# First expert's last low parts go from VectorE to GpSimd, and two table sums go behind the gathered rows

## The chip, the cores and the metric

The kernel runs on one core of one Trainium2 chip. The metric is the device time of one execution in microseconds (us), lower is better. Engines are named as the profile names them: PE (TensorE matmul), PEld (its weight loads), DVE (VectorE), ACT (ScalarE), POOL (GpSimd), SP (SyncE, which issues most DMAs).

## What is computed

Three layers in a row, all in float32, on 1536 tokens of width 512:

```python
x = attention(q, k, v)          # window of 16 keys on each side, and 24 block summaries
h = x @ w_in                    # 512 -> 2048
x2 = elu(h) @ w_out             # 2048 -> 512
logits = x2 @ w_gate            # 8 experts, each token goes to its best one
gate = softmax(logits)[best]
out[i] = gate[i] * (relu(x2[i] @ w1[e]) @ w2[e])     # e = best[i], at most 384 tokens per expert
```

Float32 products are made of "fp32r" matmuls: an operand is split into a high part (a cast, on ACT) and a low part (operand minus high part, one TENSOR_TENSOR subtraction on DVE or POOL), and three matmul passes add high x high, high x low and low x high.

## The kernel before

The tokens are taken in four tiles of 384. Attention and the two dense matmuls fill the first 350 us. Behind them come the experts, and the change lies in the stretch between, from 357 to 375 us of the profiled span. The program is written out by hand in one order for each engine: code that stands earlier is earlier in the engine's queue, and an instruction waits for the semaphores of what it reads.

Three strands run side by side there.

The first strand is the *first expert's first block*. The expert with the most tokens in the first three tiles is chosen early. Its 16 weight chunks E_0 to E_15 (128x512 each; E_0 to E_7 are of w1, E_8 to E_15 of w2) come by DMA into six `rawq` buffers, and `conv_expert` splits each: `conv_hi` is a cast on ACT (L668), `conv_lo` a subtraction (L678) on DVE, or on POOL for the chunks listed in `pool`. `Block.first` multiplies the block's rows by E_0 to E_7 (L736, tiles bh0f and bh1f), `Block.turn` transposes the result (L744) and casts its high part (L746), `turn_lo` makes its low part on DVE (L753, tile hTf), and `Block.second` multiplies by E_8 to E_15 (L760, tile yf).

The second strand is the *routing of the last tile* (`route`, a generator whose pieces are run by `next(last)`): logits (lgT, the copy ls at L523, lg), then a chain of small DVE steps on 128x24 elements that finds each token's expert (L531 to L574; `oh` at L568 marks it, `cum` at L574 counts), the matmuls pp (L581) that read `oh`, a second chain of DVE steps (L588 to L612), the matmul tp (L619), and `tab` (L626), the table of token numbers by expert and position.

The third strand is the *rest of the first expert*: from `tab` the DVE makes `gidxa`, the row numbers (L1307 to L649); POOL issues two indirect DMAs that gather those rows (L693, tile xgq); PE transposes them (L700, tile bt), ACT casts the high part (L703, tile xbq) and DVE makes the low part (L704). Then every engine loads two token counts from `regs` into registers (TENSOR_LOAD) and branches, and PE multiplies the gathered rows by E_0 and so on (L810, tile bh): first eight passes that read only the high part of xbq, then four that read its low part.

Between these, the DVE counts tokens (`count_key`, L633), sorts the other seven experts by size (L1338 to L1370, ending in `regs`), and POOL and DVE bring the table into sorted order: `by_rank(v)` is a multiplication on POOL (L1358, tile tmp), and a sum on DVE follows for each v (L1379, tile tabs). `regs` also lets SP load expert numbers and start the DMAs of the next expert's weights.

Of the kernel before, what the change touches and what calls it, by code (L numbers as in the profile page):

```python
# [49 lines left out]
def build(tc, cap, qT, kT, vT, vP, wi, wo, wg, wgT, wx, out):  # L50
# [6 lines left out]
    with ctx:  # L57
        pool = lambda **kw: ctx.enter_context(tc.tile_pool(**kw))
# [569 lines left out]
        def count_key(nm, n):  # L628

            ct = psm("ct" + nm, "T")  # L630
            nc.tensor.matmul(ct[:, 0:NE], lhsT=ones, rhs=cums[n], start=True, stop=True)
            cnt = const.tile([P, NE], F32, name="cnt" + nm)
            nc.vector.tensor_copy(cnt, ct[:, 0:NE])  # L633
            key = const.tile([P, NE], F32, name="key" + nm)
            nc.vector.tensor_scalar(out=key, in0=cnt, scalar1=float(NE), scalar2=None, op0=ALU.mult)
            nc.vector.tensor_tensor(key, key, iota_e, op=ALU.subtract)
            return cnt, key

        def slots(src, n, nm):

            gidx = const.tile([P, n], U32, name="gidx" + nm)
            nc.vector.tensor_scalar(out=gidx, in0=src[:, :, 0], scalar1=1.0, scalar2=-1.0, op0=ALU.max, op1=ALU.add)
            gate = const.tile([P, n], F32, name="gate" + nm)
            nc.vector.tensor_tensor(gate, src[:, :, 1], src[:, :, 2], op=ALU.add)
            pad = const.tile([P, n], F32, name="pad" + nm)
            nc.vector.tensor_scalar(out=pad, in0=src[:, :, 0], scalar1=0.0, scalar2=padid, op0=ALU.is_equal, op1=ALU.mult)
            nc.vector.tensor_tensor(pad, pad, src[:, :, 0], op=ALU.add)
            sidx = const.tile([P, n], U32, name="sidx" + nm)
            nc.vector.tensor_scalar(out=sidx, in0=pad, scalar1=-1.0, scalar2=None, op0=ALU.add)  # L649
            return gate, gidx, sidx  # L650
# [4 lines left out]
        NCHUNK = 16  # L655
# [3 lines left out]
        def raw_of(k, m):  # L659
            return RAW[m % NRAW] if k == 0 else RAW[((k - 1) * NCHUNK + m) % len(RAW)]  # L660

        def raw_load(k, ms):
            for m in ms:
                nc.sync.dma_start(raw_of(k, m), wx[ds(ereg[k], 1), :, m, :].rearrange("o p f -> p (o f)"))

        def conv_hi(k, ms, vec=()):
            for m in ms:
                (nc.vector.tensor_copy if m in vec else nc.scalar.copy)(EW[k][m][:, 0], raw_of(k, m))  # L668

        def conv_expert(k, ms, pool=(), vec=()):  # L670
            for m in ms:
                conv_hi(k, [m], vec)
                conv_lo(k, [m], pool)

        def conv_lo(k, ms, pool=()):
            for m in ms:
                w, raw = EW[k][m], raw_of(k, m)
                (nc.gpsimd if m in pool else nc.vector).tensor_tensor(w[:, 1], raw, w[:, 0].bitcast(F32), op=ALU.subtract)  # L678
                nxt = m + len(RAW)
                if nxt < NCHUNK:  # L680
                    raw_load(k, [nxt])
                elif 0 < k < NE - 1:
                    raw_load(k + 1, [nxt - NCHUNK])

        def alloc_expert(k):

            pl, tg = (wpool, "W") if k % 2 == 0 else (w2pool, "W2")
            EW[k] = [pl.tile([P, 2, 512], F32R, tag=tg, name=f"E{k}_{m}") for m in range(NCHUNK)]
            for i in range(k + 2, NE, 2):
                EW[i] = EW[k]  # L690
# [6 lines left out]
        def load_xT(xb, col, xg, nm):  # L697
            pt = psm("bt" + nm, "TSO"[col // P])
            for c in range(NCC):
                nc.tensor.transpose(pt[:, c * P : (c + 1) * P], xg[:, c * P : (c + 1) * P], ident)  # L700
            ptv = pt.rearrange("p (c q) -> p c q", q=P)
            q = slice(col, col + P)
            nc.scalar.copy(xb[:, 0, :, q], ptv)  # L703
            nc.vector.tensor_tensor(xb[:, 1, :, q], ptv, xb[:, 0, :, q].bitcast(F32), op=ALU.subtract)  # L704
# [169 lines left out]
        def busy(n):  # L874

            warm = pacc("warm")
            for _ in range(n):
                nc.tensor.transpose(warm[:, 0:P], ident, ident)
# [395 lines left out]
        next(last)  # L1274
        blk.first(0, 2)
        blk.first(0, 3)
        conv_expert(0, range(11, 12))
        next(last)
        blk.turn(0, lo=False)
        blk.first(1, 0)  # L1280
        conv_hi(0, range(12, NCHUNK))
        next(last)
        blk.turn_lo(0)
        blk.first(1, 1)
# [3 lines left out]
        blk.second(0)  # L1288
        blk.second(1)
        blk.turn(1, lo=False)  # L1290
        conv_lo(0, range(12, 13))
        next(last, None)
        blk.second(2)
        blk.second(3)
# [20 lines left out]
        def gathers(k, nb):  # L1315

            _, gidx, _, c0 = GS[k]
            j0 = 1 if k == 0 else 0
            for j in range(j0, min(nj, j0 + nb)):
                gather(XG[j - j0], gidx[:, c0 + j : c0 + j + 1], N)  # L1320

        def ahead(k, nb, nm=""):

            j0 = 1 if k == 0 else 0
            for i in range(min(nb, nj - j0)):
                load_xT(XB[k % 2], i * P, XG[i], f"{i}_{k}" + nm)

        GS = {0: slots(tf0.rearrange("p (j v) -> p j v", v=3), nj, "a") + (0,)}
        gathers(0, GRP)
        conv_lo(0, range(13, 14))  # L1330
        blk.turn_lo(1)
        conv_lo(0, range(14, NCHUNK))
        cnt, key = count_key("1", NT)
        for f in range(4, 8):
            blk.second(f)
# [20 lines left out]
        def by_rank(v):  # L1356
            tmp[v] = bpool.tile([P, NE, nj, NE], F32, tag="e2", bufs=2, name=f"tmp{v}")
            nc.gpsimd.tensor_tensor(  # L1358
                tmp[v], tabv[:, v].unsqueeze(1).to_broadcast([P, NE, nj, NE]),
                perm.unsqueeze(2).to_broadcast([P, NE, nj, NE]), op=ALU.mult)  # L1360
# [14 lines left out]
            RAW.append(bpool.tile([P, 512], F32, tag=f"raw{m}", name=f"rawq{m}"))  # L1375
        raw_load(1, range(NRAW2))
        alloc_expert(1)
        for v in range(3):
            nc.vector.tensor_reduce(  # L1379
                out=tabs[:, :, v].rearrange("p (k j) -> p k j", j=nj), in_=tmp[v], op=ALU.add, axis=AX.X)  # L1380
            if v == 0:
                by_rank(2)
        ysf = bpool.tile([P, DM], F32, tag="ys", bufs=3, name="ysf")
        finish(blk.y, st["slot0"][0][:, 0:1], st["slot0"][1][:, 0:1], "f", ysf)
        busy(4)
        ahead(0, GRP)
        allsl = slots(tabs, NE * nj, "1")
        for k in range(1, NE):
            GS[k] = allsl + (k * nj,)
# [141 lines left out]
```

## Time and profile before

| | |
|---|---|
| median of 3 runs | 496.82 us (495.53 to 497.0) |
| the profiled execution, its own time | 496.97 us |
| its span, first to last instruction | 495.2 us |
| instructions | 9033 |
| PE busy | 472.0 us (95% of the span) |
| DVE busy | 333.2 us (67%) |
| ACT busy | 263.5 us (53%) |
| POOL busy | 189.6 us (38%) |

The span is what the trace's clock counts from (0 is its first instruction); the execution's own time is 1.8 us longer. A row of the trace's timeline gives the start, the duration, the engine, the line, the operation, the tile written and the tiles read, the shapes, how many instructions the row merges, and in square brackets how long the engine had been idle before it and which instruction ended that.

### The profile page before, as it was taken

Reading aid. Unit: us, or ns where it says so; the run is one execution under the profiler, and the core shown is the slowest. Engines: PE = TensorE matmul, PEld = TensorE weight load, DVE = VectorE, ACT = ScalarE, POOL = GpSimd, SP = SyncE. Lnnn points to the kernel's source line nnn. Section 1 sums busy time; section 2 is a strip of 40 time slices with the busy share of each in tenths; the row PEclk is TensorE's granted clock in tenths of the full one; section 3 lists DMA queues with packets and bytes.
Section 4 is the critical chain, followed back from the end, with each engine's and each line's share of the span. In section 5 each row is a group of like instructions: output and inputs, shape, how many; then the busy total and the mean of one; then the engine's idle time right before and its main releaser. Section 6 shows DMA issues by size and latency. Waiting matters only on the chain. (4 is left out here: it accounts for less than half of the span.)

```text
span 495.2 us, 9033 instructions
## 1 busy us (share of the span) xinstructions
PE 472.0 (95%) x2996; PEld 393.0 (79%) x2996; DVE 333.2 (67%) x887; ACT 263.5 (53%) x663; POOL 189.6 (38%) x196
## 2 busy tenths in 40 slices
PE   8999999899999999999999999999998999989892
PEld 7655555688888899998999999988767889888671
DVE  4669999766755567886179889746695855356560
ACT  3656456677575555564333333435734856466440
POOL 5632334565533348886233233122524030120540
PEclk9999999999999999999999999999999999999997
DMA  8894884423424243497010000106537875376480
GB/s 260 270 311 148 242 239 113 129 89 77 149 83 122 80 176 83 142 315 269 1 64 2 31 34 1 65 0 204 147 118 233 290 226 194 115 227 215 136 271 13
DMA packets 33585, 72.85 MB, mean 147 GB/s; under 512 B 4140, under 2 KB 8940, under 8 KB 33504
## 3 DMA queue, kind: packets, MB, share of 16 engines
q1 hardware_dynamic: 31744, 66.71, 42.3%
q0 software_dynamic: 1760, 5.19, 3.5%
q8 instruction: 34, 0.56, 0.5%
q14 instruction: 47, 0.39, 0.3%
HBM read 61.88 MB, written 9.70 MB: 145 GB/s over the span
## 5 line engine op out<-in xcount | busy, mean ns | idle before, releaser
L441 PE MATMUL h<-xT,Wi 128*128 128x384 f32 x672 | 130.2, 340 | 0.0
L486 PE MATMUL acc<-Wo,g 128*128 128x512 f32 x504 | 127.2, 396 | 0.3 <-POOL g L466 0.2
L441 PEld LDWEIGHTS h<-xT,Wi 128*128 128x128 f32 x672 | 117.9, 188 | 5.8 <-issue 1.9
L466 POOL TENSOR_TENSOR g<-e,g 128x384 fp32r<-128x384 f32 x55 | 65.0, 1182 | 128.7 <-ACT g L460 128.7
L486 PEld LDWEIGHTS acc<-Wo,g 128*128 128x128 f32 x504 | 92.8, 188 | 18.3 <-POOL g L466 1.2
L453 DVE SCALAR_TENSOR_TENSOR e<-e,h 128x384 f32<-128x384 f32 x64 | 35.3, 552 | 50.9 <-ACT e L449 47.4
L448 ACT ACTIVATE e<-h 128x384 f32<-128x384 f32 x64 | 31.5, 492 | 57.6 <-PE h L441 53.9
L460 ACT CAST g<-e 128x384 fp32r<-128x384 f32 x56 | 28.8, 514 | 45.8 <-DVE e L453 45.8
L678 DVE TENSOR_TENSOR E<-rawq,E 128x512 fp32r<-128x512 f32 x70 | 46.4, 705 | 8.2 <-ACT E L668 7.0
L810 PE MATMUL bh<-xbq,E 128*128 128x256 f32 (+1 forms) x288 | 43.5, 303 | 3.6 <-issue 1.4
L810 PEld LDWEIGHTS bh<-xbq,E 128*128 128x128 f32 x288 | 41.2, 188 | 6.0 <-issue 1.8
L668 ACT CAST E<-rawq 128x512 fp32r<-128x512 f32 x75 | 42.4, 617 | 5.5 <-DMA rawq<-wx 2.9
L295 ACT ACTIVATE sc<-sc,st 128x120 f32<-128x120 f32 x96 | 36.7, 385 | 14.1 <-DVE st L288 13.9
L303 POOL TENSOR_TENSOR sc<-sc,st 128x360 f32<-128x360 f32 x32 | 27.9, 872 | 39.4 <-DVE st L302 29.1
L799 PE MATMUL y<-E,g 128*128 128x512 f32 x168 | 41.7, 393 | 0.0
L548 DVE CUSTOM_DVE_ANT_0 dot<-a,wgb 128x512 f32<-128x512 f32 x48 | 40.0, 888 | 0.0
L799 PEld LDWEIGHTS y<-E,g 128*128 128x128 f32 x168 | 30.6, 188 | 5.7
L449 ACT ACTIVATE e<-e 128x384 f32<-128x384 f32 x64 | 33.6, 525 | 2.0
L288 DVE CUSTOM_DVE_ANT_0 sc<-S,masks 128x120 f32<-128x120 f32 x96 | 21.5, 278 | 18.5 <-PE S L263 9.2
L314 ACT COPY pT<-T 120x384 f32<-120x384 f32 x32 | 15.3, 478 | 30.2 <-PE T L310 28.9
L818 DVE TENSOR_TENSOR g<-e,g 128x256 fp32r<-128x256 f32 (+1 forms) x24 | 11.3, 469 | 25.5 <-ACT g L817 21.3
L715 POOL DMA_INDIRECT out<-ys,sidx x6 | 6.3, 1053 | 48.1 <-ACT ys L714 46.7
(251 smaller groups left out, 701.1 us busy)
## 6 DMA issues: line engine op xcount, KB each, us to landing
rawq<-wx SPq DMA_DIRECT2D x88, 256.0 KB, 4.0
rawi<-wi SPq DMA_DIRECT2D x16, 512.0 KB, 4.0
rawo<-wo SPq DMA_DIRECT2D x16, 512.0 KB, 5.4
vw<-vP SPq DMA_DIRECT2D x16, 288.0 KB, 3.1
kt<-kT SPq DMA_DIRECT2D x8, 400.0 KB, 4.9
qt<-qT SPq DMA_DIRECT2D x16, 192.0 KB, 3.0
vt<-vT SPq DMA_DIRECT2D x8, 384.0 KB, 3.1
out<-xg SPq DMA_DIRECT2D x12, 256.0 KB, 4.3
```

Source lines behind the costliest of these rows:

```text
L295: nc.scalar.activation(out=sc[:, gi], in_=sc[:, gi], func=AF.Exp, bias=st[:, 0, gi : gi + 1], scale=-1.0, accum_out=st[:, 1, gi : gi + 1])
L441: nc.tensor.matmul(HP[t, f][:, 0:TT], lhsT=w[:, s, c * P : (c + 1) * P], rhs=xT[t][:, xs, c, :], start=c == 0 and n == 0, stop=c == NCC - ...
L448: nc.scalar.activation(out=e, in_=HP[t, f][:, 0:TT], func=AF.Exp)
L449: nc.scalar.activation(out=e, in_=e, func=AF.Relu, bias=1.0, scale=-1.0)
L453: nc.vector.scalar_tensor_tensor(out=e, in0=e, scalar=-1.0, in1=h[:, 0:TT], op0=ALU.mult, op1=ALU.max)
L466: eng.tensor_tensor(g[:, 1], EP.pop((t, f)), g[:, 0].bitcast(F32), op=ALU.subtract)
L486: nc.tensor.matmul(accp[tb], lhsT=g[:, s, tb * P : (tb + 1) * P], rhs=w[:, ws], start=f % FPG == 0 and n == 0, stop=f % FPG == FPG - 1 and ...
L548: nc.vector.tensor_tensor_reduce(out=junk, in0=x2[t * BPT + tb], in1=WGB[e // 2][:, e % 2], scale=1.0, scalar=0.0, op0=ALU.mult, op1=ALU.a ...
L668: (nc.vector.tensor_copy if m in vec else nc.scalar.copy)(EW[k][m][:, 0], raw_of(k, m))
L678: (nc.gpsimd if m in pool else nc.vector).tensor_tensor(w[:, 1], raw, w[:, 0].bitcast(F32), op=ALU.subtract)
L799: nc.tensor.matmul(ys[b], lhsT=g[:, s, b * P : (b + 1) * P], rhs=w[:, ws], start=f == 0 and n == 0, stop=f == 7 and n == 2)
L810: nc.tensor.matmul(h[:, 0:nt], lhsT=EW[k][half * NCC + c][:, ws, fc * P : (fc + 1) * P], rhs=xb[:, s, c, 0:nt], start=n == 0, stop=n == 3 ...
```

## The change

The low parts of chunks 11 to 15 of the first expert are made on POOL and not on DVE. Those of 12 to 15, which stood at three later places of DVE's queue, are now written right behind their casts, and so lie on POOL ahead of the gathers. Of the three sums over the sorted table, the second and third are written behind `ahead(0, GRP)`, which makes the gathered rows' low parts.

```diff
         blk.first(0, 3)
-        conv_expert(0, range(11, 12))
+        conv_expert(0, range(11, 12), pool=range(NCHUNK))
         next(last)
         blk.turn(0, lo=False)
         blk.first(1, 0)
-        conv_hi(0, range(12, NCHUNK))
+        conv_expert(0, range(12, NCHUNK), pool=range(NCHUNK))
         next(last)
...
         blk.turn(1, lo=False)
-        conv_lo(0, range(12, 13))
         next(last, None)
...
         gathers(0, GRP)
-        conv_lo(0, range(13, 14))
         blk.turn_lo(1)
-        conv_lo(0, range(14, NCHUNK))
         cnt, key = count_key("1", NT)
...
-        for v in range(3):
+
+        def ranked(v):
             nc.vector.tensor_reduce(
                 out=tabs[:, :, v].rearrange("p (k j) -> p k j", j=nj), in_=tmp[v], op=ALU.add, axis=AX.X)
-            if v == 0:
-                by_rank(2)
+
+        ranked(0)
+        by_rank(2)
...
         ahead(0, GRP)
+        ranked(1)
+        ranked(2)
         allsl = slots(tabs, NE * nj, "1")
```

The first place is POOL's queue, from the last low part that it already made (E_10) to the gathers of the first expert's rows (xgq). The queue before:

```order
L678 TENSOR_TENSOR E_9_3819<-rawq_3801,E_9_3819 128x512 [waits DMAHW5_49,Activation_49]
L678 TENSOR_TENSOR E_10_3820<-rawq_3802,E_10_3820 128x512 [waits DMAHW6_49,Activation_49]
L693 DMA xgq_4189<-x2d,gidxa 128x512 [waits DMAHW5_49,DMAHW6_49,DMAHW4_49,DVE_49]
L693 DMA xgq_4190<-x2d,gidxa 128x512
L1358 TENSOR_TENSOR tmp_4236<-tab,perm 128x192 [waits DVE_49]
```

The same queue of the changed kernel:

```order
L678 TENSOR_TENSOR E_10_3820<-rawq_3802,E_10_3820 128x512 [waits DMAHW6_49,Activation_49]
L678 TENSOR_TENSOR E_11_3821<-rawq_3803,E_11_3821 128x512 [waits DMAHW7_49,PE_49,Activation_49]
L678 TENSOR_TENSOR E_12_3822<-rawq_3798,E_12_3822 128x512 [waits DMAHW0_49,PE_49,Activation_49]
L678 TENSOR_TENSOR E_13_3823<-rawq_3799,E_13_3823 128x512 [waits DMAHW1_49,PE_49,Activation_49]
L678 TENSOR_TENSOR E_14_3824<-rawq_3800,E_14_3824 128x512 [waits DMAHW2_49,PE_49,Activation_49]
L678 TENSOR_TENSOR E_15_3825<-rawq_3801,E_15_3825 128x512 [waits DMAHW3_49,PE_49,Activation_49]
L693 DMA xgq_4192<-x2d,gidxa 128x512 [waits DMAHW5_49,DMAHW6_49,DMAHW4_49,DVE_49]
```

Five subtractions of 128x512 now stand in front of the two gathers, each waiting for its own cast on ACT and for its raw chunk.

The second place is DVE's queue at the start of the last tile's routing, in the queue before: behind the low parts of the routing's input (xh) comes the chunk's low part, then the copy of the logits (ls) and the chain of small steps that each wait for the one ahead.

```order
L514 TENSOR_TENSOR xh_4028<-xt_4043,xh_4028 128x4x128 [waits Activation_49]
L678 TENSOR_TENSOR E_11_3821<-rawq_3803,E_11_3821 128x512 [waits DMAHW7_49,Activation_49]
L523 COPY ls_4068<-lgT_4059 16x384 [waits PE_49]
L531 TENSOR_REDUCE L_4088<-lg_4084 128x24 [waits PE_49]
L557 CAST rv_4027<-tokid 128x3
L561 TENSOR_REDUCE sm_4091<-L_4088 128x3 [waits DVE_49]
L563 TENSOR_TENSOR cand_4093<-L_4088,sm_4091 128x24 [waits DVE_49]
L565 TENSOR_TENSOR cand_4093<-cand_4093,wt_e 128x24 [waits DVE_49]
L566 TENSOR_REDUCE sm_4091<-cand_4093 128x3 [waits DVE_49]
L568 TENSOR_TENSOR oh_4097<-wt_e,sm_4091 128x24 [waits DVE_49]
L571 TENSOR_TENSOR L_4088<-L_4088,sm_4091 128x24
L574 TENSOR_TENSOR cum_117<-cum_116,cs_4099 128x8 [waits DVE_49]
```

In the changed kernel the row of E_11 is gone from there and the others keep their order; in the same way E_12 is gone from ahead of tab, E_13 from ahead of hTf, and E_14 and E_15 from behind it.

The third place is DVE's queue behind the register table (regs), where the gathered rows' low parts (xbq) are made. The changed kernel:

```order
L1367 CAST regs<-srt 128x16 [waits DVE_49]
L1377 TENSOR_REDUCE tabs<-tmp_4236 128x24 [waits Pool_49]
L704 TENSOR_TENSOR xbq_4195<-bt_0_4307,xbq_4195 128x4x128 [waits Activation_49]
L704 TENSOR_TENSOR xbq_4195<-bt_0_4314,xbq_4195 128x4x128 [waits Activation_49]
L1377 TENSOR_REDUCE tabs<-tmp_4238 128x24 [waits Pool_49]
L1377 TENSOR_REDUCE tabs<-tmp_4295 128x24 [waits Pool_49]
```

Before, all three sums stood between regs and the two rows of xbq (as L1370, L1379 and L704).

## Rows read from the trace of the kernel before

**Rows 1.** The page's second part: TensorE's granted clock in 40 equal slices, in tenths.
```profile
PEclk9999999999999999999999999999999999999997
```

**Rows 2.** Timeline from 370 us: regs, transposes, gathered rows, the first matmuls behind.
```profile
370.60 1.04 PE L700 MATMUL bt<-ident,xgq 128*128 128x128 f32 x8
...
371.23 1.07 ACT L703 CAST xbq<-bt 128x512 fp32r<-128x512 f32 x2 [0.18 <-PE bt L700]
...
371.61 0.23 DVE L1370 CAST regs<-srt 128x16 int32<-128x16 f32 x1
...
373.03 1.20 PE L810 MATMUL bh<-xbq,E 128*128 128x256 f32 x8 [1.40 <-DVE tabs L1379]
373.15 1.28 DVE L704 TENSOR_TENSOR xbq<-bt,xbq 128x512 fp32r<-128x512 f32 x2
...
374.48 3.61 PE L810 MATMUL bh<-xbq,E 128*128 128x256 f32 x28 [0.24 <-DVE xbq L704]
```

**Rows 3.** Timeline from 359 to 368 us: casts, low parts, gathers, the wait for hTf.
```profile
359.12 2.23 ACT L668 CAST E<-rawq 128x512 fp32r<-128x512 f32 x4
...
364.21 0.68 DVE L678 TENSOR_TENSOR E<-rawq,E 128x512 fp32r<-128x512 f32 x1
...
364.81 0.23 DVE L626 TENSOR_TENSOR tab<-tp,tab 128x72 f32<-128x72 f32 x1
...
366.11 0.96 POOL L693 DMA_INDIRECT xgq<-x2d,gidxa  x1 [8.16 <-DVE pada L646]
...
367.02 0.68 DVE L753 TENSOR_TENSOR hTf<-ht1f,hTf 128x512 fp32r<-128x512 f32 x1
367.37 0.94 POOL L693 DMA_INDIRECT xgq<-x2d,gidxa  x1 [0.30 <-issue]
367.62 1.28 DVE L678 TENSOR_TENSOR E<-rawq,E 128x512 fp32r<-128x512 f32 x2
...
367.75 2.57 PE L760 MATMUL yf<-E,hTf 128*128 128x512 f32 x10 [1.05 <-DVE hTf L753]
```

**Rows 4.** The gathered tile xgq, 360 to 392 us: from a gather's issue to its landing.
```profile
DMA to landing us min/median/max: 3.5/3.5/3.5
```

**Rows 5.** Timeline from 357.9 to 361.3 us: the start of the routing chain.
```profile
357.94 0.69 DVE L678 TENSOR_TENSOR E<-rawq,E 128x512 fp32r<-128x512 f32 x1 [1.04 <-ACT E L668]
...
358.55 0.54 DVE L523 COPY ls<-lgT 16x384 f32<-16x384 f32 x1
...
359.24 0.26 PEld L527 LDWEIGHTS lg<-ident,ls 16*128 16x128 f32 x3 [0.37 <-DVE ls L523]
...
360.09 0.18 DVE L563 TENSOR_TENSOR cand<-L,sm 128x24 f32<-128x24 f32 x1
...
360.74 0.18 DVE L568 TENSOR_TENSOR oh<-wt_e,sm 128x24 bf16<-128x24 f32 x1
...
361.17 0.17 DVE L574 TENSOR_TENSOR cum<-cum,cs 128x8 bf16<-128x8 bf16 x1
```

**Rows 6.** POOL's timeline, 336 to 358 us: low parts E_6 to E_10 in one run.
```profile
351.66 6.29 POOL L678 TENSOR_TENSOR E<-rawq,E 128x512 fp32r<-128x512 f32 x5 [3.18 <-ACT E L668]
```

**Rows 7.** Timeline, 332 to 339 us: small DVE steps that meet a POOL subtraction.
```profile
332.14 1.01 POOL L466 TENSOR_TENSOR g<-e,g 128x384 fp32r<-128x384 f32 x1 [4.41 <-ACT g L460]
332.16 1.02 DVE L591 TENSOR_SCALAR sm<-sm 128x3 f32<-128x3 f32 x1
...
337.86 1.01 POOL L466 TENSOR_TENSOR g<-e,g 128x384 fp32r<-128x384 f32 x1 [4.70 <-ACT g L460]
337.92 0.96 DVE L644 TENSOR_TENSOR gate<-ts 128x1 f32<-128x1 f32 x1
```

**Rows 8.** Line L591, all four executions: duration in ns, least, median, most.
```profile
L591 DVE TENSOR_SCALAR sm<-sm x4: 157/164/1017, 279.6 to 362.1; 128x3 f32<-128x3 f32 x4
```

**Rows 9.** Timeline, 294 to 297 us: back-to-back DVE dot products around a POOL subtraction.
```profile
294.75 0.69 DVE L548 CUSTOM_DVE_ANT_0 dot<-a,wgb 128x512 f32<-128x512 f32 x1
294.85 1.46 POOL L466 TENSOR_TENSOR g<-e,g 128x384 fp32r<-128x384 f32 x1 [2.73 <-ACT g L460]
...
295.36 1.50 DVE L548 CUSTOM_DVE_ANT_0 dot<-a,wgb 128x512 f32<-128x512 f32 x1
```

## The prediction

> **What bounds the kernel now.** I started with TensorE's granted clock over the whole span: full in every slice but the last [rows 1], so nothing in the middle needs a clock to explain it. PE is busy 95% of the span, so an edit of this size can only be worth what PE waits in its own stretch. Reading the timeline there backwards from the end of the stretch, the reader should see three waits of PE. At 374.48 the low passes of the gathered rows begin, after the DVE's last xbq low part, which runs 373.15 to 374.43 [rows 2]. At 373.03 the high passes begin, 1.40 us after PE had its last transpose; their data are ready at 372.30 (end of the ACT casts), but PE must first load two counts and branch, and `regs` is written only at 371.84: 373.03 - 371.84 = 1.19 us for loads and branch [rows 2]. At 367.75 PE resumes yf after 1.05 us, on the low part of hTf, which stands behind E_13 in DVE's queue [rows 3]. From 374.48 on PE runs nearly without gaps; I take every shift of that instant as a shift of the end.
>
> So I follow one number, t, the start of the low passes (374.48), and make the sum against the profiled execution's 496.97 us.
>
> **What sets t afterwards.** The gathers are issued at 366.11 and 367.37 and land 3.5 us later [rows 3, 4]: the second at 370.87, just ahead of its transposes (the second half of the group that ran 370.60 to 371.64). Before, t was 3.61 us behind that landing, because `regs`, the three sums and the DVE were late. In the changed kernel E_14 and E_15 no longer stand ahead of the counts (1.28 us [rows 3]) nor two of the sums ahead of xbq, so regs and the low parts are early and only the landing counts: landing, transposes and cast of the second block (0.57 + 0.1 + 0.55, from the halves of the rows of bt and xbq), which the 1.19 us of loads and branch about equal: 1.25 us; then 1.20 us of high passes [rows 2]. With x for the shift of the gathers, t = 370.87 + x + 2.45, and the end moves by **x - 1.16 us**. That 1.16 us is the gain that the later edits bring, and it also says how late the gathers may become before all is lost.
>
> **x, part one: DVE steps removed.** Without E_11 (0.69 us at 357.94) the copy ls starts when its matmul is done, some 0.34 us before 358.55; PE waited 0.37 us for it, so the whole routing chain starts 0.37 us earlier [rows 5]. Without E_12 (364.21 to 364.89) the sum tab, at 364.81, starts on its matmul's end instead, 0.12 us earlier [rows 3]. Together -0.49 us.
>
> **x, part two: POOL's five low parts beside the chain.** POOL does one in 6.29 / 5 = 1.26 us [rows 6]. E_11 runs 357.95 to 359.2, beside DVE steps that read PSUM, and costs nothing. E_12 waits for its cast, the first of four from 359.12 at 2.23 / 4 = 0.56 us each, so it starts at 359.74; E_12 to E_15 need at least 5.04 us and end at 364.8 or later. The gathers come after that even with the chain early, so POOL's queue as such delays nothing.
>
> What does cost is that DVE and POOL exclude each other. At 332.16 a DVE step on 128x3 elements that takes 0.16 us elsewhere took 1.02, from just behind the start of a POOL subtraction to its end; at 337.92 one on 128x1 took 0.96 beside another [rows 7, 8]. And the exclusion alternates: a POOL subtraction issued at 294.85 beside back-to-back dot products took 1.46 us against 1.01, since it waited for the dot product in hand, but the one behind that then waited for POOL until 296.31 and ended at 296.86 [rows 7, 9]. The Trainium skill, page "SBUF — State Buffer", section "Who interferes with whom", says why: a VectorE instruction with two SBUF inputs and a GpSimd instruction that reads SBUF want one shared port pair, whoever issues first has it for the whole instruction and the other blocks; reductions and steps with one PSUM input are free. The rows above agree with the blocking; no row shows five small steps against four POOL instructions in a row. By the rule the sum is the one I make next, and by a mere sharing of bandwidth it would be rival one.
>
> From 359.72 on, the chain's steps that take two tiles from SBUF are L563, L565, L568, L571 and L574, each 0.17 or 0.18 us and at most a reduction apart (their old places run from 360.09 to 361.17 [rows 5]). Each finds POOL in an instruction, waits for its end, runs, and POOL's next one starts in the 0.2 us or so before the next step is issued. Worked through, with E_12 just ahead of L563: L563 after 361.0, E_13 from 361.1, L565 after 362.35, E_14 from 362.45, L568 after 363.7, E_15 from 363.8, L571 after 365.06, L574 at 365.4. With L563 just ahead of E_12 the last is 365.15. Before, L574 stood at 361.17. So it is 4.0 to 4.2 us late instead of 0.37 early, and by then POOL is done, so the rest of the chain runs at its old pace. Queued behind it: `oh` is late for the pp matmuls (PE idles from about 361.2 to 363.9), hTf's first half for E_8's third pass, then tab, gidxa and the gathers. x = 4.1 - 0.12 = **+4.0 us**. Bounds: at least three POOL instructions are met in full before the hTf step, which reads PSUM and runs beside the last (x about 3.2); at most four at 1.29 with 0.18 between them (x about 4.3).
>
> **Other paths.** PE's yf: hTf's low part moves to 370.4, so yf's ten matmuls end at 373.7, and transposes start with the landing at 374.85 for the second block, not earlier. regs: counts follow hTf, 371.0 + 3.0 us of sorting as before = 374.0, ahead of the branch at 375.0; the SP loads of the next weights move by +2.2 us, less than PE, so they stay covered. The sums moved behind xbq give row numbers for the next expert's gathers, wanted 13 us later: nothing.
>
> **The sum.** x - 1.16 = 4.0 - 1.16 = +2.8 us: 496.97 + 2.8 = 499.8, and against the median, 0.15 us under the profiled execution, **499.7 us**. With the bounds of x (3.2 to 4.3) and 0.3 us either way for the landing and the loads: 498.7 to 500.3.
>
> **Rivals.** One: the small steps slip past POOL (sharing, or DVE served at once). Then x = -0.49, the sum -1.65, 495.2 us. For it: the stretch's DVE steps are short, and POOL is idle there now, so no row of this chain meets it. Against: rows 7. It decides between one and two POOL instructions met: break-even is x = 1.16, or 1.65 us of waiting against 1.26 for one. Two: partial blocking, one or two instructions met, because DVE keeps the ports over neighbouring steps or POOL starts late: x from 0.6 to 2.0, 496.3 to 497.7. Three: worse than the sum. PE now idles for 2.7 us around 362 and again at hTf; if the granted clock fell there to 1.2 of 2.4 GHz, the fifteen matmuls behind (0.26 us each [rows 3]) would take up to 3.9 us more, of which some 1 us lies beside DVE's chain: 500.7 to 502.7. Nothing in rows 1 shows it.
>
> **How the numbers follow.** About 0.3%, 1.5 us, is what a measurement of this kernel can tell from no change. The sum as worked out: 0.72. Rival one 0.11, two 0.10, three 0.07. Rival one lies at the edge of "faster" (495.3), so I give it 0.08 there and the rest to "same", with rival two. Slower 0.80, same 0.12, faster 0.08. The likeliest case's own range is 498.7 to 500.3; the stated one reaches down to rival two's upper end and up into rival three: 497.5 to 501.2.
>
> **What the profile after would show.** Right: L563, L565, L568, L571 or L574 with durations around 1.2 us in place of 0.18, each ending with a POOL L678; POOL's E_12 to E_15 one after another until 365; L574 near 365.3; pp near 363 to 364; gathers near 370.1 and 371.4; no DVE sum between regs and xbq; low passes near 377.3. Wrong: the same steps at 0.18 us beside a busy POOL (rival one), or t moved by other than x - 1.16, which would put the error in the landing or the loads. The forecast fails if DVE's chain passes more than two of the four POOL instructions unhindered.

## The result and the profile after

The changed kernel takes 500.36 us (median of 16 runs) against 497.28 for the kernel before (16 runs): ratio 1.0069, 95% interval 1.0054 to 1.0085. It is slower by 3.4 us by the ratio (0.0069 x 497.28; the medians are 3.1 apart), where the forecast was 2.9 and 499.7 us. The profiled execution took 501.25 us, with a span of 499.4.

The changed kernel's timeline from 355 to 382 us (start, duration, engine, line, operation, tiles, shapes, idle time before and what ended it):

```profile
358.04 0.55 DVE L523 COPY ls<-lgT 16x384 f32<-16x384 f32 x1 [1.30 <-PE lgT L521]
...
359.07 0.26 PEld L527 LDWEIGHTS lg<-ident,ls 16*128 16x128 f32 x3 [0.36 <-issue]
...
359.66 4.98 POOL L678 TENSOR_TENSOR E<-rawq,E 128x512 fp32r<-128x512 f32 x4 [0.55 <-ACT E L668]
359.92 1.09 DVE L563 TENSOR_TENSOR cand<-L,sm 128x24 f32<-128x24 f32 x1
361.04 1.18 DVE L565 TENSOR_TENSOR cand<-cand,wt_e 128x24 f32<-128x24 f32 x1
362.26 0.18 DVE L566 TENSOR_REDUCE sm<-cand 128x3 f32<-128x24 f32 x1
362.47 0.97 DVE L568 TENSOR_TENSOR oh<-wt_e,sm 128x24 bf16<-128x24 f32 x1
363.37 1.31 DVE L571 TENSOR_TENSOR L<-L,sm 128x24 f32<-128x24 f32 x1
363.50 0.17 PE L581 MATMUL pp<-oh,tri 128*128 128x8 bf16 x1 [2.48 <-DVE oh L568]
...
364.80 0.17 DVE L574 TENSOR_TENSOR cum<-cum,cs 128x8 bf16<-128x8 bf16 x1
...
368.21 0.70 PE L619 MATMUL tp<-B,A 128*128 128x72 f32 x3
...
368.95 0.23 DVE L626 TENSOR_TENSOR tab<-tp,tab 128x72 f32<-128x72 f32 x1 [1.02 <-PE tp L619]
...
370.25 0.96 POOL L693 DMA_INDIRECT xgq<-x2d,gidxa  x1 [5.61 <-DVE pada L646]
370.56 0.68 DVE L753 TENSOR_TENSOR hTf<-ht1f,hTf 128x512 fp32r<-128x512 f32 x1
371.30 2.57 PE L760 MATMUL yf<-E,hTf 128*128 128x512 f32 x10 [0.33 <-DVE hTf L753]
371.51 0.94 POOL L693 DMA_INDIRECT xgq<-x2d,gidxa  x1 [0.31 <-issue]
373.95 0.25 DVE L1367 CAST regs<-srt 128x16 int32<-128x16 f32 x1
375.06 0.63 PE L700 MATMUL bt<-ident,xgq 128*128 128x128 f32 x4 [0.32 <-DMA xgq<-x2d,gidxa]
...
376.36 4.58 PE L810 MATMUL bh<-xbq,E 128*128 128x256 f32 x36 [0.67 <-ACT xbq L703]
```

Read it against [rows 2, 3, 5]. POOL makes E_12 to E_15 in one run from 359.66 to 364.64, and in just that stretch four of the five DVE steps with two SBUF inputs take 0.97 to 1.31 us in place of 0.18. The reduction L566 keeps its 0.18 between them. `oh` (L568) is late, so PE stands idle for 2.48 us at pp. L574 is at 364.80 where it was at 361.17, the first gather at 370.25 where it was at 366.11. On the other side the later edits do what was worked out: the 36 passes of bh now run in one piece from 376.36, without a wait for xbq's low part inside, and regs (373.95) is no longer what they wait for.

The matmuls lgT, ahead of all this, start 0.16 us earlier in the execution of after than in that of before (357.14 against 357.30); shifts measured from them:

| | before, us behind lgT | after | shift |
|---|---|---|---|
| ls copied | 1.25 | 0.90 | -0.35 |
| lg's weight load | 1.94 | 1.93 | 0 |
| L574 | 3.87 | 7.66 | +3.79 |
| tab | 7.51 | 11.81 | +4.30 |
| first gather | 8.81 | 13.11 | +4.30 |
| end of bh's 36 passes | 20.79 | 23.80 | +3.01 |

Between L574 and tab there is 4.15 us against 3.64. The changed kernel's windows (stretch, length, PE, PEld, DVE, ACT and POOL busy with their counts, granted clock, DMA share, GB/s) show why:

```profile
360.00:364.00 4.00, 1.52 (x15) 1.08 (x14) 3.90 (x5) 1.14 (x3) 4.00 (x4) 1.00 0.24 91
364.00:368.00 4.00, 3.50 (x12) 2.44 (x11) 3.89 (x23) 0.71 (x2) 0.64 (x1) 0.65 0.02 4
368.00:372.00 4.00, 3.67 (x18) 2.71 (x17) 2.74 (x14) 0.59 (x1) 1.44 (x2) 0.92 0.02 8
```

Behind the wait for `oh`, which left PE 1.52 us of work in 4 us, the granted clock falls to its lower level, 1.2 of 2.4 GHz: 0.65 and 0.92 mean (1 - 0.65) x 2 x 4 = 2.8 us and 0.6 us at half speed. The matmuls tp, which end the second chain of small steps, come late by that.

In absolute times the end of bh is 3.01 - 0.16 = 2.85 us late, and from there the shift stays: y's group at 456.89 stands at 454.06 before. What the profiled execution loses beyond that lies at the end. PE's timeline of the changed kernel, 440 to 505 us:

```profile
456.89 4.36 PE L799 MATMUL y<-E,g 128*128 128x512 f32 x18
463.10 6.00 PE L736 MATMUL bh<-E,xbq 128*128 128x512 f32 x18 [1.85 <-issue]
```

The same matmuls of the kernel before, in the same view:

```profile
459.82 4.43 PE L736 MATMUL bh<-E,xbq 128*128 128x512 f32 x18 [1.40 <-issue]
```

A second fall of the clock stands here (granted clock 0.65 from 463 to 467 us): the 18 matmuls take 1.57 us more, with 0.45 us more of idling ahead of them. Some of it is made up again behind them: the whole span is 4.2 us longer, not 2.85 + 1.57 + 0.45. The second fall is also seen where E_11 to E_15 stay on DVE (first experiment), so I don't count it to the change.

### The profile page after: what moved, and what is told of

Read it like the earlier page. It is cut to its first block, busy times and chain, and to the rows that moved or that the text cites. A ratio compares the mean times of both kernels' runs of the same rounds, so it can differ in the third digit from the quotient of the medians.

```text
span 499.4 us, 9036 instructions
## 1 busy us (share of the span) xinstructions
PE 474.4 (95%) x2996; PEld 394.9 (79%) x2996; DVE 334.7 (67%) x882; ACT 263.5 (53%) x663; POOL 195.7 (39%) x201
## 5 line engine op out<-in xcount | busy, mean ns | idle before, releaser
L678 DVE TENSOR_TENSOR E<-rawq,E 128x512 fp32r<-128x512 f32 x65 | 44.4, 727 | 8.4 <-ACT E L668 7.2
```

## The experiments

All were timed beside the kernel before on the same chip; its median was 496.88 us with the first four and 497.82 with the others (35 runs each).

### The two sums alone

The kernel before, with only the sums moved:

```diff
-        for v in range(3):
+        def ranked(v):
...
+        ranked(0)
+        by_rank(2)
...
         ahead(0, GRP)
+        ranked(1)
+        ranked(2)
```

> The kernel before with only the second part of the change: two of the three sums behind the gathered rows' low parts, all low parts of the weights on DVE. Theory: PE still waits for regs plus 1.19 us of loads and branch, then runs 1.20 us of high passes, and finds the low parts ready: the low passes start 0.25 us earlier, 497.0 us, which is no difference that can be told. Rival (the low parts of the rows were the wait that counted): 0.7 us or more earlier.

Measured: 495.73 us, ratio 0.9974 [0.9951, 0.9997]. The end of bh's 36 passes moves by -0.52 us from lgT. Its timeline, 366 to 380 us:

```profile
372.14 0.23 DVE L1370 CAST regs<-srt 128x16 int32<-128x16 f32 x1
...
372.55 1.27 DVE L704 TENSOR_TENSOR xbq<-bt,xbq 128x512 fp32r<-128x512 f32 x2
...
373.56 4.57 PE L810 MATMUL bh<-xbq,E 128*128 128x256 f32 x36 [1.28 <-DVE xbq L704]
```

xbq's low part follows regs by 0.41 us in place of 1.54 [rows 2], and the 36 passes run in one piece; their start does not move (15.70 us behind lgT against 15.73), since it hangs on regs: 373.56 - 372.37 = 1.19 us of loads and branch, as before. What is gained lies inside the passes, which take 4.57 us from first to last in place of 374.48 + 3.61 - 373.03 = 5.06 [rows 2]. That is twice the 0.25 us expected: the wait of 0.24 us is gone, and besides the two pieces took 1.20 + 3.61 = 4.81 us [rows 2] where the one takes 4.57. The medians lie 1.15 us apart, and the interval nearly takes in none; what goes beyond the 0.52 us no row shows. The profiled execution also has the second fall of the clock (the same 18 matmuls in 5.99 us), though nothing of the first expert was changed here.

### The five low parts alone

The changed kernel with the three sums put back in their old place.

```diff
-        ranked(0)
-        by_rank(2)
+        for v in range(3):
...
+            if v == 0:
+                by_rank(2)
...
-        ranked(1)
-        ranked(2)
```

> The changed kernel with its second part undone: low parts 11 to 15 on POOL, but the three sums in one piece ahead of the gathered rows' low parts, as in the kernel before. Theory (the loss is all in the low parts, and the sums' place matters only where regs is late): the time of the changed kernel, 500 to 500.8 us, at most 0.3 us above it. Rival (the sums' new place costs or gains a part of the difference): more than 1 us away from the changed kernel.

Measured: 500.16 us, ratio 1.0058 [1.0035, 1.0081]. The steps wait as in the changed kernel: L574 stands at 7.66 us behind lgT, as there, the first gather at 13.18. Timeline:

```profile
375.39 4.58 PE L810 MATMUL bh<-xbq,E 128*128 128x256 f32 x36 [0.68 <-ACT xbq L703]
```

bh waits for ACT's cast, not for the DVE: with the gathers this late the place of the sums hardly matters (the end of bh at 24.03 against 23.80). The loss lies in the low parts on POOL.

### POOL subtractions that nobody needs

The kernel before, with all low parts where they were, and four POOL subtractions of the same size added at the same place, on the same inputs, into a spare tile that nobody reads.

```diff
         conv_hi(0, range(12, NCHUNK))
+        spare = mpool.tile([P, 512], F32R, tag="t1", bufs=T1, name="spare")
+        for m in range(12, NCHUNK):
+            nc.gpsimd.tensor_tensor(spare, raw_of(0, m), EW[0][m][:, 0].bitcast(F32), op=ALU.subtract)
```

> The kernel before, with four POOL subtractions of 128x512 added where the changed kernel has those of chunks 12 to 15; they read the same tiles and write a tile that nobody reads, so every low part stays on DVE. Theory (POOL's instructions hold up the small DVE steps that read two SBUF tiles): L563, L565, L568 and L571 take 0.95 to 1.35 us instead of 0.18, L574 and the gathers come about 3.8 us later, and since nothing is taken off DVE the whole of it reaches the end: 500.5 to 502 us, +3.5 to +4.5 on the kernel before. Rival (the loss comes from something else that the change does to the low parts or to the order behind them): same as before, 497.3 us, with all steps at 0.18 us.

Measured: 500.68 us, ratio 1.0071 [1.0046, 1.0096]. Timeline:

```profile
360.53 5.41 POOL L1284 TENSOR_TENSOR spare<-rawq,E 128x512 fp32r<-128x512 f32 x4 [1.85 <-ACT E L668]
...
360.79 1.09 DVE L563 TENSOR_TENSOR cand<-L,sm 128x24 f32<-128x24 f32 x1
361.91 0.18 DVE L565 TENSOR_TENSOR cand<-cand,wt_e 128x24 f32<-128x24 f32 x1
...
362.34 0.92 DVE L568 TENSOR_TENSOR oh<-wt_e,sm 128x24 bf16<-128x24 f32 x1
...
363.51 1.09 DVE L574 TENSOR_TENSOR cum<-cum,cs 128x8 bf16<-128x8 bf16 x1
```

Nothing waits for these four results, and no DVE work was taken away, yet the same kind of steps wait: it is POOL's subtractions that hold them, not the move. Only three of the five are held here; the last subtraction meets a TENSOR_SCALAR of the second chain instead (L591, 0.64 us). The four subtractions write one tile and take 5.41 us against 4.98, and L565 passes at 0.18 us right behind L563, which fits a gap between the first and the second. The gathers are +2.99 us late, and the median is 3.8 us up, of which the trace lays 3.0 at bh.

### POOL writes in place of reads

As before, but POOL only fills the spare tile (13 memsets, 7.52 us), so that it is busy over the whole chain without reading SBUF.

```diff
         conv_hi(0, range(12, NCHUNK))
+        spare = mpool.tile([P, 512], F32, tag="t1", bufs=T1, name="spare")
+        for m in range(13):
+            nc.gpsimd.memset(spare, 0.0)
```

> The kernel before, with thirteen POOL memsets of 128x512 added at the same place, some 7 us of POOL work that writes SBUF and reads none; nobody reads the tile. Theory (only POOL instructions that read SBUF hold up DVE's second input): the small steps L563 to L574 stay at 0.17 to 0.18 us beside a busy POOL, and the time is that of the kernel before within 0.3%, 496.3 to 498.3 us. Rival (any POOL work on SBUF holds up DVE): the steps take up to 0.5 us each, L574 comes 1.5 to 3 us later, 498.8 to 500.3 us.

Measured: 497.85 us, ratio 1.0002 [0.9977, 1.0028]. Timeline:

```profile
358.32 7.52 POOL L1284 MEMSET spare<- 128x512 f32 x13
...
360.17 0.44 DVE L557 CAST rv<-tokid 128x3 fp32r<-128x3 f32 x1
...
360.67 0.18 DVE L563 TENSOR_TENSOR cand<-L,sm 128x24 f32<-128x24 f32 x1
360.89 0.18 DVE L565 TENSOR_TENSOR cand<-cand,wt_e 128x24 f32<-128x24 f32 x1
...
361.32 0.18 DVE L568 TENSOR_TENSOR oh<-wt_e,sm 128x24 bf16<-128x24 f32 x1
...
362.64 0.30 DVE L591 TENSOR_SCALAR sm<-sm 128x3 f32<-128x3 f32 x1
```

Beside a POOL that only writes, the two-input steps keep 0.18 us, though a memset lasts 0.58 us and a step held by one would show it. So it takes a POOL instruction that reads SBUF, as the subtractions do, to hold them. One thing I had not expected: casts and TENSOR_SCALAR steps of 128x3 elements do wait (0.44 and 0.30 us; L591 takes 0.16 elsewhere [rows 8]), and the gathers come 0.68 us late by that, and so does the end of bh. The medians lie 1.0 us apart, but the ratio's interval takes in none.

The Trainium skill, page "SBUF — State Buffer", section "Who interferes with whom", says both: a VectorE step with two SBUF inputs collides with a GpSimd instruction that reads SBUF and not with one that only writes, while copies, casts and tensor_scalar can run in a mode that takes both port pairs and collide with GpSimd whatever it does. The rows of this run and the one before it agree on both counts.

### Only E_11, and the sums

```diff
-        conv_expert(0, range(11, 12))
+        conv_expert(0, range(11, 12), pool=range(NCHUNK))
```

and the sums as in the first experiment; E_12 to E_15 stay on DVE.

> The kernel before with the sums in their new place and only chunk 11's low part on POOL; those of 12 to 15 stay on DVE. It asks whether POOL's first instruction is free and whether the copy ls, now earlier, starts the routing chain earlier. Theory: POOL's instruction ends before L563, all small steps at 0.18 us; lg does not come earlier than before, since in the changed kernel it stood at the same place with ls 0.48 us ready, so the time is that of the sums alone, 495.5 to 496.5 us, 0.2 to 0.3% under the kernel before. Rival (the chain does start 0.37 us earlier, as the prediction had it): another 0.35 us less, with lg 0.37 us earlier against lgT.

Measured: 496.42 us, ratio 0.9971 [0.9951, 0.9991]. Timeline:

```profile
358.10 1.28 POOL L678 TENSOR_TENSOR E<-rawq,E 128x512 fp32r<-128x512 f32 x1 [0.36 <-ACT E L668]
358.30 0.55 DVE L523 COPY ls<-lgT 16x384 f32<-16x384 f32 x1 [1.29 <-PE lgT L521]
...
359.32 0.26 PEld L527 LDWEIGHTS lg<-ident,ls 16*128 16x128 f32 x3 [0.36 <-issue]
...
360.18 0.18 DVE L563 TENSOR_TENSOR cand<-L,sm 128x24 f32<-128x24 f32 x1
```

E_11 on POOL costs nothing, as forecast, and gains nothing either: `ls` ends at 358.85, 0.47 us ahead of the weight load that reads it, and that load still starts 1.92 us behind lgT, as in the kernel before (1.94). The sums alone give the gain (the end of bh at 20.29 us behind lgT, against 20.27 with the sums alone). By its interval this version is faster than the kernel before, and so than the changed one: 1.4 us under the kernel before, of which the trace shows 0.5; the rest no row explains.

### The changed kernel with PE kept at work

Twenty small matmuls that nobody reads, put into PE's queue ahead of pp, in the changed kernel:

```diff
         blk.first(1, 2)
+        busy(20)
         next(last)
```

> The changed kernel with 20 idle transposes put on PE ahead of the pp matmuls, so that PE works through most of its 2.5 us wait for oh. It asks what the lower granted clock behind that wait costs. Theory (the clock fell because PE stood idle there, and at half clock tp came late for tab): the granted clock stays full from 360 to 372 us, tab and the gathers come 0.3 to 0.6 us earlier against L574, and the time is 0.3 to 1.2 us under the changed kernel, 499.2 to 500.0 us, still slower than before. Rival (the low clock is hidden beside DVE's chain): the time of the changed kernel, 500.3 us.

Measured: 500.4 us, ratio 1.0054 [1.0029, 1.0079]. The granted clock is 1.00 in all three windows from 360 to 372 us. Timeline:

```profile
361.72 2.35 PE L878 MATMUL warm<-ident 128*128 128x128 f32 x20
...
364.39 0.17 PE L581 MATMUL pp<-oh,tri 128*128 128x8 bf16 x1 [0.32 <-DVE oh L568]
...
365.70 0.17 DVE L574 TENSOR_TENSOR cum<-cum,cs 128x8 bf16<-128x8 bf16 x1
...
368.68 0.50 PE L619 MATMUL tp<-B,A 128*128 128x72 f32 x3 [0.53 <-DVE B L612]
...
369.22 0.23 DVE L626 TENSOR_TENSOR tab<-tp,tab 128x72 f32<-128x72 f32 x1 [0.39 <-PE tp L619]
```

The lock is unchanged (L574 at 7.70 us behind lgT), but L574 to tab is 3.52 us in place of 4.15, tp's three matmuls 0.50 in place of 0.70, the gathers 0.59 us earlier than in the changed kernel, and the end of bh 0.41 us earlier (+2.60 on before). So in the trace the slow clock is worth about half a microsecond here. The time expected, 499.2 to 500.0 us, was missed: the two medians are the same, and the scatter of the runs is too wide to show half a microsecond.

### Two of the four on POOL

E_11, E_12 and E_13 on POOL, E_14 and E_15 on DVE as before, and the sums moved:

```diff
-        conv_hi(0, range(12, NCHUNK))
+        conv_expert(0, range(12, 14), pool=range(NCHUNK))
+        conv_hi(0, range(14, NCHUNK))
...
-        conv_lo(0, range(12, 13))
...
-        conv_lo(0, range(13, 14))
```

> The changed kernel with only chunks 11, 12 and 13 on POOL; 14 and 15 stay on DVE behind hTf's low part. It asks whether the loss goes by the number of POOL instructions that the chain meets. Theory: two of them are met, L563 and L565 take about 1.1 us each, L568 and L571 0.18; L574 and the gathers come 1.8 to 2.0 us later, PE waits 0.7 us for oh and keeps its clock, and by x - 1.16 the low passes start 0.6 to 0.9 us later than before: 497.5 to 498 us. Rival (any POOL work there costs the whole): 500 us or more.

Measured: 498.85 us, ratio 1.0015 [0.9991, 1.0039]. Timeline, and behind it the window around the end of PE's wait:

```profile
359.75 2.52 POOL L678 TENSOR_TENSOR E<-rawq,E 128x512 fp32r<-128x512 f32 x2 [0.54 <-ACT E L668]
360.00 1.07 DVE L563 TENSOR_TENSOR cand<-L,sm 128x24 f32<-128x24 f32 x1
361.11 1.19 DVE L565 TENSOR_TENSOR cand<-cand,wt_e 128x24 f32<-128x24 f32 x1
...
362.55 0.18 DVE L568 TENSOR_TENSOR oh<-wt_e,sm 128x24 bf16<-128x24 f32 x1
...
362.78 0.17 PE L581 MATMUL pp<-oh,tri 128*128 128x8 bf16 x1 [1.68 <-DVE oh L568]
```

```profile
364.00:368.00 4.00, 4.00 (x15) 3.34 (x14) 2.67 (x20) 1.18 (x2) 0.00 (x0) 0.57 0.02 4
```

Two subtractions hold two steps, L574 is 1.88 us late: the price goes by the POOL instruction met. That the clock would hold, which I had expected, was wrong: PE's wait of 1.68 us is followed by a mean clock of 0.57. The gathers come 2.62 us late, and the end of bh 1.52 us, both more than expected. The ratio gives 0.7 us (the medians 1.0) with an interval that includes none; the time expected was 497.5 to 498.

### hTf's low part ahead of E_13

The version of the fifth experiment, with hTf's low part ahead of E_13 on DVE.

```diff
-        conv_lo(0, range(13, 14))
         blk.turn_lo(1)
-        conv_lo(0, range(14, NCHUNK))
+        conv_lo(0, range(13, NCHUNK))
```

> A version meant to beat both: the sums in their new place, chunk 11's low part on POOL, and hTf's low part ahead of chunk 13's on DVE, so that PE resumes yf 0.6 us earlier. Theory: PE's wait for hTf shrinks from 1.05 to about 0.4 us, but the low passes still wait for regs plus loads and branch, which do not move, so it is the time of the sums alone, 495.5 to 496.5 us. Rival (yf's end counts as well): a further 0.4 to 0.6 us less.

Measured: 497.18 us, ratio 0.9984 [0.9962, 1.0006]. Timeline:

```profile
366.50 2.71 PE L760 MATMUL yf<-E,hTf 128*128 128x512 f32 x10 [0.44 <-DVE hTf L753]
...
372.35 4.57 PE L810 MATMUL bh<-xbq,E 128*128 128x256 f32 x36 [1.48 <-DVE xbq L704]
```

PE's wait of 1.05 us [rows 3] shrinks to 0.44, and bh starts where it did (15.69 us behind lgT): the time is only handed to the wait behind, which regs ends. The median lies above the 495.5 to 496.5 us expected, and 0.8 us above the fifth experiment's with the same end of bh (20.26 us behind lgT), which fits the scatter of such medians (the two intervals overlap). Of the waits of PE in this stretch, only the one that ends last is worth anything.

## Why the prediction was right, and where its terms were off

**The mechanism.** Four of DVE's five small two-input steps each waited out a POOL subtraction, as the prediction worked it through, and t moved by x less about 1.16 us: x - shift of the end was 1.29 in the changed kernel, 1.11 with PE kept at work, 1.10 with two on POOL. Rivals one and two (steps slip past, or only one or two are met) fell with the first rows; the runs with subtractions that nobody needs and with memsets show that POOL's reading instructions hold the steps, not its being busy nor the move as such.

**Part one of x was mis-sized.** The prediction gave -0.37 us for the earlier `ls`. The copy did come 0.35 us earlier, but the weight load of lg did not (1.93 us behind lgT in the changed kernel and 1.92 with E_11 alone, against 1.94, though `ls` was ready 0.47 us ahead). The prediction says that PE waited 0.37 us for `ls`, but that row of [rows 5] is PEld's; PE itself was at work. The matmuls queued ahead of lg, first in the kernel before, then in the changed one:

```profile
358.36 0.95 PE L736 MATMUL bh1f<-E,xb 128*128 128x512 f32 x3
```

```profile
358.20 0.94 PE L736 MATMUL bh1f<-E,xb 128*128 128x512 f32 x3
```

They end at 359.31 and 359.14, and lg's load starts 0.07 us ahead of that end in both (0.07 or 0.08 in every run here), whether `ls` was ready 0.15 us before the load, as in the kernel before, or 0.48. With `ls` early, the same 0.36 us of PEld stands there as "issue". So the trace named `ls`, but by these rows what lg still waited for was PE's own work. No run moved bh1f to test it.

**The lock was a little cheaper.** The four waits beyond the steps' own 0.18 us are 0.91 + 1.00 + 0.79 + 1.13 = 3.83 us. The prediction's 4.0 to 4.2 late from a start 0.37 early is 4.4 to 4.6. The held steps end at 361.01, 362.22, 363.44 and 364.68, 1.22 us apart; the prediction had them 1.35 apart, since it let POOL's next subtraction start only behind the step. POOL ran its four at 4.98 / 4 = 1.25 us, as if alone [rows 6].

**A term was missing.** The granted clock fell behind the 2.48 us of idling at pp, which is the first half of rival three. Rows 1 could not warn of it, since PE has no such wait in the kernel before (busy for all of 360 to 364 us). Its price is 0.63 us of the small steps' chain (4.15 against 3.52, the value with PE kept at work) and 0.41 us at the end of bh, not rival three's 1 to 3: most of the slow matmuls lie beside DVE's chain, and the granted clock is 1.00 again from 372 us, ahead of bh.

That the sum came out so near is in part luck, since the three errors nearly cancel in x: L574 came 3.79 us late for 4.1, and from there to tab it took 0.51 us more in place of 0.12 less, +4.30 in all for +4.0. At the end of bh the changed kernel is 3.01 us late for a forecast of 2.8, and 2.85 with the earlier start of this execution. (One slip in the range: 499.7 less 0.8 and 0.3 is 498.6, not 498.7.)

**The rest of 3.4 us.** Part the runs of each kernel by their mean granted clock, between 0.993 and 0.994. Beside the first four experiments, 16 of the 35 runs of the kernel before are at 0.994 to 0.996 and average 496.36 us; the other 19 average 498.09. Of the changed kernel's 16 runs, two are at 0.995 and 0.996 (499.50 and 499.13 us), and the other 14, at 0.990 or below, average 500.84. Group by group the difference is 2.95 us (from two runs only) and 2.75 us, close to the forecast's 2.8. The rest of 3.4 comes from the mix: more of the changed kernel's runs are in the lower group. That the two falls of the clock put them there fits the profiled execution, but only one execution of the changed kernel has a trace; how often each fall occurs, and whether the change makes the second more frequent, is open.

## What to carry to other kernels

- An idle engine is not a free one: work put on GpSimd beside a chain of small, dependent VectorE steps can cost the chain most of one GpSimd instruction for each step with two SBUF inputs, as long as GpSimd has instructions that read SBUF (0.74 to 1.13 us here on a step of 0.18). Place such work where VectorE reads PSUM or reduces (E_11 cost nothing). Shorter GpSimd pieces might cost less for each step met; no run tried that.
- Work behind a late transfer is worth moving only up to the next thing that ends last; work out that limit first (here 1.16 us), since it also says how much lateness undoes the gain.

## What the runs showed of the hardware

- POOL memsets of 128x512, 0.58 us each, let VectorE's two-input steps pass at 0.18 us, but held casts and TENSOR_SCALAR steps of 128x3 elements to 0.30 to 0.47 us, where the latter take 0.16.
- In the profiles the granted clock fell to its lower level behind waits of PE of 2.48 us (twice: the changed kernel and the low parts alone) and 1.68 us at pp, not behind one of 1.42 at the same place, nor where 20 small matmuls filled the wait.
- Behind the branch between experts, PE's "issue" wait at about 461 us is followed by a second fall in some kernels' profiles (the changed kernel, the sums alone, the dummy subtractions, two on POOL; waits of 1.85 to 2.15 us) and not in the others' (1.29 to 1.92 us), so the length of the wait alone does not decide it; the 18 matmuls there take 6.0 us or 4.4 to 4.6 of PE's time.
- lg's weight load started 0.36 us ("issue") after PEld's last one though its operand had been ready 0.47 us; the three matmuls ahead of it on PE ended 0.07 us later. A wait that a trace puts down to an operand can have a second cause right under it.
